# Two of the sixteen last stores of a fused attention and expert kernel begun from GpSimd's queue

## Chip, cores, metric

One core of a Trainium2 chip. The metric is the device time of one execution in microseconds (us). The profile's span (first to last recorded instruction) is about 1.8 us shorter than it (496.21 and 494.4 for the profiled run before), and all times in views are counted from the span's start.

## The reference, cut

```python
def _attn_ref(q, k, v):                     # q, k, v: (8, 8, 576, 64)
    q_p, k_p = phi(q), phi(k)               # phi(x) = elu(x) + 1
    kv = np.einsum('bhsd,bhse->bhde', k_p, v)
    num = np.einsum('bhsd,bhde->bhse', q_p, kv)
    den = np.einsum('bhsd,bhd->bhs', q_p, k_p.sum(2))[..., None] + 1e-06
    return num / den

def _moe_ref(x, domain_probs, w1, w2):      # x: (4608, 512), 4 experts of 512 -> 1024 -> 512
    p = domain_probs / (domain_probs.sum(-1, keepdims=True) + 1e-09)
    out = 0
    for e in range(4):
        out += p[:, e:e + 1] * (np.maximum(x @ w1[e], 0.0) @ w2[e])
    return out                              # (4608, 512) float32
```

## The kernel before, where the change touches it

Each batch has 576 tokens: four blocks of 128 and 64 left over. The left-over tokens of the eight batches form a ninth group of 512 tokens, the last "unit" with expert 3. Its second layer is seven products per half of the tokens (`p`, in the order 1, 2, 6, 5, 7, 3, 4; `i` is 0 or 1). Each product ends in one VectorE sum into `acc`. Products 2, 7, 3 and 4 complete a quadrant of the output: 128 tokens by 256 of the 512 columns. A quadrant holds rows of two batches, so it is stored by two DMAs of 64 partitions, one on SyncE's queue and one on ScalarE's: sixteen stores of 64 KB in all.

```python
    def store(j, ns, cols=slice(0, Dm)):
        acc = accs[j, ns][:, cols]
        if j < B:
            ...                              # whole blocks, on SyncE alone
        else:
            for u in range(2):
                (nc.scalar if u else nc.sync).dma_start(
                    out=out_b[2 * ns + u, SM:S, cols],
                    in_=acc[u * HP : (u + 1) * HP],      # HP = 64
                )

    def layer2_product(j, e, h, hss, p, i):
        ...                                  # 4 matmuls into PSUM
        add_acc(j, e, ns, ps, ds, first and e == 0)      # VectorE
        if (j, e) == (NTILES - 1, E - 1):
            if p in (2, 3, 4, 7):
                store(j, ns, ds)
```

## Time and profile before

| | before |
|---|---|
| median of the first 3 runs (all) | 495.89 us (495.54 to 497.17) |
| span of the profiled run, granted share of the full TensorE clock | 494.4 us, 1.0 |
| VectorE's last sum ends | 490.00 us |
| ScalarE's last store begins, lands | 491.32, 493.33 us |
| from VectorE's last end to the span's end ("the tail") | 4.4 us |

The lines that carry this stand in the prediction below. A line of the timeline such as `488.02 3.85 ACTq ... x6` merges six store issues of ScalarE's queue, from the first one's beginning at 488.02 over 3.85 us to the last one's end. Time in such a line is issue, not the transfer.

### The profile page before, as it was taken

To read this page: it belongs to the slowest core of one execution; us is meant where nothing else is said; L and a number is where in the kernel's file an instruction comes from. 1 tells how busy PE (TensorE), PEld (TensorE's weight loads), DVE (VectorE), ACT (ScalarE), POOL (GpSimd) and SP (SyncE) were. 2 spreads that over 40 slices of the span, in tenths; PEclk is the share of its full clock that TensorE was granted. 3 is DMA by queue.
4 is the path that set the end of the run, shared out by engine and by line. 5 is a ranking of instruction groups with operands and counts; after the bars stand their busy time and mean duration, and the time that the engine had idled before them with its cause. 6 is when DMAs were issued, how large, how long until landed. Compare 5 with 4: busy or idle time off the path is not lost.

```text
span 494.4 us, 11616 instructions
## 1 busy us (share of the span) xinstructions
PE 483.2 (98%) x4346; PEld 409.4 (83%) x4346; DVE 378.7 (77%) x802; ACT 336.2 (68%) x678; POOL 354.2 (72%) x339
## 2 busy tenths in 40 slices
PE   8999989999999999999999999999999999999995
PEld 3556656888898989898989898989898888888884
DVE  5757987798967987698859886888687756775686
ACT  5777969964978498848894789468954565446530
POOL 3735204778967797769776977698669877987774
PEclk9999999999999999999999999999999999999999
DMA  8999976542345235533464245523241020002003
GB/s 253 215 219 239 272 140 177 172 104 52 121 162 130 55 111 164 131 66 95 137 160 82 71 150 139 101 60 93 81 78 30 5 95 1 1 2 86 1 1 87
DMA packets 82201, 53.66 MB, mean 109 GB/s; under 512 B 46240, under 2 KB 75936, under 8 KB 82144
## 3 DMA queue, kind: packets, MB, share of 16 engines
q1 hardware_dynamic: 70592, 40.07, 30.7%
q0 software_dynamic: 9824, 11.27, 12.1%
q10 hardware_dynamic: 1728, 1.57, 1.2%
q8 instruction: 34, 0.56, 0.5%
q14 instruction: 23, 0.19, 0.1%
HBM read 45.16 MB, written 9.44 MB: 110 GB/s over the span
## 4 chain that ended last, share of the span: by engine, by line
PE 78%; DMA 12%; DVE 3%; ACT 3%; POOL 2%; issue 1%; SPq 0%; ACTq 0%; DVEq 0%; POOLq 0%
PE py L668 37%; PE pb L733 21%; PE pe L733 16%; DMA w<-in_moe_w_dram 7%; DMA rawu<-in_q_dram 2%; DVE acc L570 1%; PE psum_nd L465 1%; DMA rawb<-in_v_dram 1%; PE psum_kv L425 1%; PE py L579 1%; DMA out_dram<-acc 1%; DMA rawh<-in_q_dram 1%; POOL w L183 1%; PE pb L668 1%; DVE x_sb L448 1%
## 5 line engine op out<-in xcount | busy, mean ns | idle before, releaser
L570 DVE SCALAR_TENSOR_TENSOR acc<-py,p_sb,acc 128x256 f32<-128x256 f32 (+1 forms) x382 | 182.3, 488 | 49.4 <-PE py L668 40.1
L717 DVE CUSTOM_DVE_ANT_0 h<-pe,u 128x512 f16<-128x512 f32 x140 | 96.3, 688 | 42.0 <-PE pe L733 25.2
L733 PEld LDWEIGHTS <-w 128*128 128x128 f16 x1120 | 108.8, 98 | 17.0 <-issue 1.8
L635 POOL TENSOR_TENSOR hs<-h 128x512 f16<-128x512 f16 x64 | 73.9, 1155 | 55.2 <-DVE h L717 54.0
L668 PEld LDWEIGHTS <-h 128*128 128x128 f16 x1024 | 99.6, 98 | 12.3 <-issue 1.0
L668 PE MATMUL py<-w,h 128*128 128x256 f16 x744 | 106.4, 273 | 0.3 <-ACT acc L568 0.3
L744 ACT COPY u<-pb 128x512 f32<-128x512 f32 x140 | 82.7, 590 | 27.4 <-PE pb L733 25.8
L637 POOL TENSOR_TENSOR hs<-hs,h 128x512 f16<-128x512 f16 x64 | 74.6, 1166 | 27.2 <-PE py L668 24.6
L733 PEld LDWEIGHTS <-s 128*128 128x128 f16 x840 | 81.6, 98 | 11.4 <-DVE s L607 0.2
L733 PE MATMUL pb<-tt,w 128*128 128x256 f16 x560 | 84.0, 273 | 0.8 <-ACT u L744 0.7
L668 PEld LDWEIGHTS <-hs 128*128 128x128 f16 x768 | 74.4, 98 | 9.9 <-issue 1.3
L641 POOL TENSOR_TENSOR hs<-h,hs 128x512 f16<-128x512 f16 x64 | 74.4, 1162 | 3.5 <-PE py L668 2.9
L668 PE MATMUL py<-t,hs 128*128 128x256 f16 x496 | 74.4, 272 | 0.6 <-DVE acc L570 0.4
L639 POOL TENSOR_TENSOR h<-h 128x512 f16<-128x512 f16 x64 | 74.4, 1162 | 0.0
L759 ACT ACTIVATE h<-pe 128x512 f16<-128x512 f32 x70 | 41.9, 598 | 45.0 <-PE pe L733 44.5
L753 ACT COPY pe<-pb 128x512 f32<-128x512 f32 x70 | 40.2, 575 | 41.5 <-PE pb L733 14.9
L777 ACT ACTIVATE h<-pb 128x512 f16<-128x512 f32 x70 | 41.9, 599 | 10.0 <-PE pb L733 9.9
L733 PE MATMUL pb<-tt,s 128*128 128x256 f16 x280 | 42.0, 273 | 0.0
L733 PE MATMUL pe<-tt,s 128*128 128x256 f16 x280 | 42.0, 273 | 0.0
L733 PE MATMUL pb<-xT,w 128*128 128x256 f16 x248 | 37.2, 273 | 0.1
L733 PE MATMUL pe<-xT,w 128*128 128x256 f16 x248 | 37.2, 273 | 0.0
L733 PE MATMUL pe<-xT,s 128*128 128x256 f16 x248 | 37.2, 273 | 0.0
(120 smaller groups left out, 604.9 us busy)
## 6 DMA issues: line engine op xcount, KB each, us to landing
out_dram<-acc SPq DMA_DIRECT2D x32, 256.0 KB, 2.5
w<-in_moe_w_dram POOLq DMA_DIRECT2D x14, 512.0 KB, 13.0
rawb<-in_v_dram SPq DMA_DIRECT2D x26, 256.0 KB, 2.7
rawb<-in_q_dram SPq DMA_DIRECT2D x26, 256.0 KB, 2.7
rawb<-in_k_dram SPq DMA_DIRECT2D x26, 256.0 KB, 3.1
w<-in_moe_w_dram POOLq DMA_DIRECT2D x4, 256.0 KB, 5.8
rawb<-in_k_dram POOLq DMA_DIRECT2D x4, 256.0 KB, 11.1
rl<-in_q_dram SPq DMA_DIRECT2D x16, 64.0 KB, 2.5
```

The lines of the kernel that those rows point to most:

```text
L570: nc.vector.scalar_tensor_tensor(out=acc, in0=ps, scalar=pscal, in1=acc, op0=AO.mult, op1=AO.add)
L635: nc.gpsimd.tensor_tensor(out=hs[0], in0=a21, in1=a22, op=AO.add)
L637: nc.gpsimd.tensor_tensor(out=hs[1], in0=hs[0], in1=a11, op=AO.subtract)
L639: nc.gpsimd.tensor_tensor(out=a21, in0=a11, in1=a21, op=AO.subtract)
L641: nc.gpsimd.tensor_tensor(out=hs[3], in0=a12, in1=hs[1], op=AO.subtract)
L668: nc.tensor.matmul(out=ps, lhsT=lhsT(k), rhs=rhs[:, k], start=first and k == 0, stop=k == FH - 1, skip_group_check=True,)
L717: nc.vector._custom_dve(TENSOR_ADD_SAT, out=out, in0=ps, in1=u, s0=BIG, s1=0.0)
L733: nc.tensor.matmul(out=ps[:, kk], lhsT=lk(kc), rhs=rhs[:, kc], start=first and kk == 0 and kc == 0, stop=kc == 1, skip_group_check=True,)
L744: nc.scalar.copy(u, self.b)
L753: nc.scalar.copy(self.e5, self.b)
L759: nc.scalar.activation(self.h[:, :, 0, 0:NH], self.e5, AF.Relu)
L777: nc.scalar.activation(self.h[:, :, 1, 0:NH], self.b, AF.Relu)
```

## The change

Its intent: at the end the two hardware queues are behind VectorE, so one quadrant is taken off both and given to GpSimd, which is idle by then.

```diff
-    def store(j, ns, cols=slice(0, Dm)):
+    def store(j, ns, cols=slice(0, Dm), engs=(nc.sync, nc.scalar)):
@@
             for u in range(2):
-                (nc.scalar if u else nc.sync).dma_start(
+                engs[u].dma_start(
@@
             if p in (2, 3, 4, 7):
-                store(j, ns, ds)
+                store(j, ns, ds, *([(nc.gpsimd,) * 2] if (p, i) == (7, 1) else ()))
```

The built programs differ in nothing else: seven stores instead of eight on SyncE and on ScalarE, two new ones at the end of GpSimd's stream.

## The prediction

> **What bounds the kernel now.** I read the page's busy table first, then the timeline of the last ten microseconds, then the store issues one queue at a time, then the landings and SyncE's own waits.
>
> ```profile
> span 494.4 us, 11616 instructions
> PE 483.2 (98%) x4346; PEld 409.4 (83%) x4346; DVE 378.7 (77%) x802; ACT 336.2 (68%) x678; POOL 354.2 (72%) x339
> ```
>
> TensorE is busy in 98% of the span, so for some 489 us only TensorE's work counts. The change touches nothing there: the comparison of the two built programs finds TensorE's and VectorE's instruction streams identical. What can move is the tail after the last matmul. Its timeline, first VectorE's end, then the two store queues, each read again from a later moment so that the merged line splits:
>
> ```profile
> 489.08 0.92 DVE L570 SCALAR_TENSOR_TENSOR acc<-pb,p_sb,acc 128x256 f32<-128x256 f32 x2
> ...
> 485.22 6.29 SPq L557 DMA_DIRECT2D out_dram<-acc  x8
> 487.84 3.68 SPq L557 DMA_DIRECT2D out_dram<-acc  x6
> 490.97 0.55 SPq L557 DMA_DIRECT2D out_dram<-acc  x1
> ...
> 485.23 6.64 ACTq L557 DMA_DIRECT2D out_dram<-acc  x8
> 488.02 3.85 ACTq L557 DMA_DIRECT2D out_dram<-acc  x6
> 491.32 0.55 ACTq L557 DMA_DIRECT2D out_dram<-acc  x1
> ```
>
> The last sums are written at 490.00 (489.08 + 0.92). ScalarE's queue begins its last store only at 491.32, so it is 1.3 us behind the data. From the third store (488.02) to the eighth (491.32) are five steps: 3.30 / 5 = 0.66 us each; on SyncE 3.13 / 5 = 0.63. The issue itself takes 0.55 us, the rest is a wait instruction and gaps. VectorE delivers a quadrant every 0.44 us (two of 0.48, overlapping, in 0.92), so in this stretch the queues are the slower side. They hold the tail.
>
> ```profile
> L557 SPq DMA_DIRECT2D out_dram<-acc x4: 547/550/552, 489.0 to 491.0; - x4
> L557 ACTq DMA_DIRECT2D out_dram<-acc x4: 552/552/559, 489.4 to 491.3; - x4
> ...
> DMA to landing us min/median/max: 2.0/2.0/2.1
> ...
> SPq L1023 <- DMA out_dram<-acc: 1.5, 3, 0.6
> ```
>
> These are the last four stores of each queue: 2.0 us from issue to landing, with no growth from first to last, so the DMA engines are not backed up. The last lands at 491.32 + 2.01 = 493.33 (the trace's completion stamp), and SyncE's closing waits follow it (the last line). From there to the span's end it is 494.4 - 493.3 = 1.1 us of closing waits and barriers.
>
> The path of the end is therefore: VectorE's quadrants, ScalarE's queue at 0.66 us a store, 2.0 us of landing, 1.1 us of closing.
>
> **What the Trainium skill says.** "DMA: Bandwidth & Descriptors", section "Issuing engines are not separate DMA queues": all three issuers run on the same 16 DMA engines, and a second issuer saves only the time that a sequencer takes to initiate. That is just what is short here: 0.55 us of issue against 0.44 us of production. In "Latency and other measured facts" the same page gives a first byte after about 1 us for software descriptors and about 0.6 us for hardware ones. The trace agrees with the second: in steady state the first packet follows the end of a store's issue by 0.65 us. For GpSimd it is slower than stated: the first GpSimd load began at 10.43, took 0.91 us, and the software queue's first packet is at 12.78, 2.35 us after the start, though on DMA engines that other loads kept full. "Perfetto Trace Analysis", section "DMA Instruction — SWDGE (GPSIMD)": the recorded end of such an instruction is the end of descriptor writing, not of the data. I count it so.
>
> **The change, part by part.** The fourth of the eight quadrants in store order (the second token block of product 7) moves. Its two halves of 64 partitions x 256 columns (64 KB each) leave SyncE and ScalarE, which keep seven stores each, and go one after the other to GpSimd, whose last compute ends at 487.13 (485.97 + 1.16) and which is then free.
>
> - Removed: one store from each hardware queue. ScalarE's third store stays at 488.02 to 488.63. The next is now the first quadrant of product 3, whose data are complete at 488.69 (the end of the fourth record before the end; 490.00 less three steps of 0.44), so it begins at about 488.71: queue and data meet. Four stores remain, three steps of 0.65 after it: 488.71 + 1.95 = 490.66 for the last, against 491.32. That is 0.66 us gained; its landing goes from 493.33 to about 492.67. SyncE's last comes to 490.64, so both queues end together.
> - Added: two issues on GpSimd. Their data are complete at 488.25. GpSimd's load issues of 64 KB (the leftover rows) took 0.63 to 0.65 us, the first issue of the run 0.91. From 488.30 I take 0.91 and 0.65: ends at 489.2 and 489.85. First packets 1.44 us later (12.78 - 11.34, from the one case above): 490.65 and 491.3. From first packet to landing a steady store takes 0.8 us (492.53 to 493.33): landings at 491.45 and 492.1. This is an estimate, and about 0.6 us of slack to 492.67.
> - Moved: completion counters. The hardware stores use eight counters in turn; with 14 stores instead of 16 the last ones fall on counters that SyncE checks earlier in its closing series. Each check takes 0.06 us, and about two more now stand after the last landing: +0.12 us.
> - Contention: in the steady part the DMA engines are 0.90 busy at 204 GB/s (490.0 to 491.9), and two stores are to be fitted into a tail that is shorter by 0.66 us. Early in the run they moved 340 GB/s, so busy is not full, but I allow 0.1 us.
>
> Sum: -0.66 + 0.12 + 0.1 = -0.44 us, so a span of 494.0 and, taken from the median, 495.89 - 0.44 = 495.45 us. That is 0.1% of the time.
>
> **Rivals.**
>
> - GpSimd's stores become the last to land. Each queue's first two stores after a rest landed 3.1 to 3.6 us after issue, against 2.0 later, and ScalarE's second issue lasted 2.09 us. A rested software queue may pay the same: 1.4 us more puts its landings at 492.85 and 493.5, past the hardware's 492.67 and even past the old 493.33. The end would then be the same or up to 0.4 us later: 495.9 to 496.3. GpSimd idles from 487.13 and has issued no DMA since about 52 us, which speaks for this; that the 2.35 us already came from a first use on full engines speaks against. I give it 35%.
> - The issue is not the limit, the DMA engines are (0.90 busy). Then fewer stores per queue bring no earlier end, since the bytes are the same: 495.9. Against it speaks the constant 2.0 us to landing; a backed-up engine would make it grow. 10%.
> - Everything meets: no contention, no extra closing checks, the full 0.66 us: 495.2. 15%.
>
> What is left, 40%, is the main line. All of these lie within 0.15% of each other's neighbour; the spread of the three runs before (495.54 to 497.17) is larger than any of them.
>
> **Range and chances.** The cases run from 495.2 to 496.3; with the runs' scatter, 494.7 to 496.7. Two per cent would be 9.9 us. The whole tail after the last matmul is about 5 us, so faster by 2% is excluded, and slower by 2% would need something outside the tail or the slow luck of one chip. Faster 0.005, same 0.985, slower 0.01.
>
> **What would show it.** In the changed profile: seven stores a queue, ScalarE's last beginning near 490.66 with a landing of 2.0; two GpSimd issues from about 488.3, of 0.6 to 0.9 us; a software-queue row with 128 KB in the tail, first packet near 490.6; the last TensorE and VectorE records where they were. Wrong would be: a landing of the GpSimd stores after 492.7; landings of the hardware stores growing beyond 2.1 us (contention); a closing of clearly more than 1.2 us (GpSimd's own drain or counters); a third hardware store later than 488.1, which would mean that the slow second issue on ScalarE changed too.

## The result, and the profile after

| | before | after |
|---|---|---|
| median of 6 runs each (all) | 496.06 us (495.54 to 497.17) | 496.14 us (495.65 to 496.37) |
| five rounds: median | 496.17 us of 9 | 495.87 us of 5 |
| tail, profile of the first job / second profile | 4.44 / 4.42 us | 4.09 / 4.13 us |

The ratio of after to before is 0.9998 (95% interval 0.9985 to 1.0011) in the first job and 0.9989 (0.9976 to 1.0003) in the five rounds. A ratio is the mean time of one kernel's fast runs over that of the other's of the same rounds, so it is not quite the ratio of the medians quoted. Kernels are compared only within the same rounds.

The page of the changed kernel, first lines; TensorE is as busy as before:

```profile
span 494.2 us, 11615 instructions
...
PE 483.7 (98%) x4346; PEld 409.7 (83%) x4346; DVE 378.4 (77%) x802; ACT 336.6 (68%) x678; POOL 355.8 (72%) x341
```

The timeline of its last microseconds, with the two hardware queues each read from more than one moment (start, length, engine, what, how many):

```profile
489.21 0.92 DVE L570 SCALAR_TENSOR_TENSOR acc<-pb,p_sb,acc 128x256 f32<-128x256 f32 x2
488.68 1.13 POOL L557 DMA_DIRECT2D out_dram<-acc  x2 [1.41 <-DVE acc L570]
487.98 3.27 SPq L557 DMA_DIRECT2D out_dram<-acc  x5
490.69 0.56 SPq L557 DMA_DIRECT2D out_dram<-acc  x1
487.98 3.58 ACTq L557 DMA_DIRECT2D out_dram<-acc  x5
488.85 0.52 ACTq L557 DMA_DIRECT2D out_dram<-acc  x1
489.47 0.77 ACTq L557 DMA_DIRECT2D out_dram<-acc  x1
491.00 0.56 ACTq L557 DMA_DIRECT2D out_dram<-acc  x1
```

VectorE ends at 490.13 (489.21 + 0.92), 0.13 us later than in the profile before, so I count from there. ScalarE's last store begins at 491.00, 0.87 us after VectorE's end; before it was 1.32. Two things in these lines were not forecast. GpSimd begins its first store at 488.68, though its data were complete at 488.38 (the end of a VectorE sum). And one of ScalarE's issues, at 489.47, takes 0.77 us where 0.55 is usual.

The landings of the stores still at issue after 489.6, from the view of the output tensor (us from issue to landing):

```profile
DMA to landing us min/median/max: 2.0/2.3/2.5
```

In the kernel before the last eight stores landed 2.0 to 2.1 us after issue; here they take 2.0 to 2.5. The last hardware store is again a 2.02 (to 493.02); the longer ones come before it. GpSimd's two landed 1.95 and 2.40 us after issue, at 490.63 and 491.64. Their rows went out in 32 packets of 4096 bytes in all, where one store of a hardware queue took 64 of 1024 bytes. The Trainium skill, "DMA: Bandwidth & Descriptors", section "Anatomy of one DMA — SWDGE (gpsimd) path", gives about 2.0 us of fixed cost for a software DMA; these landings agree.

From the trace's completion stamps, the tail is this sum, in us after VectorE's last end:

```
                  last store begins   lands    closing until the span's end   tail
before                 1.32           3.33              1.11                  4.44
after                  0.87           2.89              1.20                  4.09
```

So the tail is 0.35 us shorter in the first pair of profiles, and 0.29 in the second pair (4.42 and 4.13).

### The profile page after: what moved, and what is told of

Its sections match the earlier page's. It is cut to its first block, busy times and chain, and to the rows that moved or that the text cites. A ratio compares the mean times of both kernels' runs of the same rounds, so it can differ in the third digit from the quotient of the medians.

```text
span 494.2 us, 11615 instructions
## 1 busy us (share of the span) xinstructions
PE 483.7 (98%) x4346; PEld 409.7 (83%) x4346; DVE 378.4 (77%) x802; ACT 336.6 (68%) x678; POOL 355.8 (72%) x341
## 3 DMA queue, kind: packets, MB, share of 16 engines
q10 hardware_dynamic: 1648, 1.51, 1.1%
## 4 chain that ended last, share of the span: by engine, by line
PE 81%; DMA 10%; DVE 3%; ACT 3%; POOL 1%; issue 1%; DVEq 0%; POOLq 0%; ACTq 0%
PE py L668 38%; PE pb L733 22%; PE pe L733 16%; DMA w<-in_moe_w_dram 7%; DMA rawu<-in_q_dram 2%; PE warm_ps L860 1%; PE psum_nd L465 1%; DMA rawb<-in_v_dram 1%; PE psum_kv L425 1%; DVE acc L570 1%; DVE x_sb L448 1%; PE pb L668 1%; PE py L579 0%; ACT u L744 0%; ACT psum_ee L315 0%
## 5 line engine op out<-in xcount | busy, mean ns | idle before, releaser
L668 PE MATMUL py<-w,hs 128*128 128x256 f16 x248 | 37.2, 273 | 0.0
```

The lines of the kernel that those rows point to most:

```text
L668: nc.tensor.matmul(out=ps, lhsT=lhsT(k), rhs=rhs[:, k], start=first and k == 0, stop=k == FH - 1, skip_group_check=True,)
```

## Experiments

My theory A, after the result: the tail is a chain of issues on the hardware queues, 2.0 us of landing and a closing series (SyncE's checks of the completion counters, then barriers of all engines); the change shortens the chain, by less than forecast; and 0.3 us is too small to be seen in whole runs. The rivals: the shorter tail is luck; the DMA engines and not the issues are the limit; GpSimd's stores slow the hardware queues.

Times below are in us after VectorE's last end in the same trace unless a clock time is meant. A queue's "step" is the time from the beginning of one issue to the beginning of the next.

**before_again**: no edit.

> The kernel before, unchanged, for a second profile: how far the tail (from VectorE's last end to the span's end, 4.4 us in the first profile) repeats on its own, and where the scatter of whole runs (495.5 to 497.2) lies. Theory A (the tail is a fixed chain of issues; the scatter is earlier, in the loads of the first microseconds): tail 4.3 to 4.5 us, the last store's issue 1.3 us after VectorE's end. Rival (the tail itself scatters by as much as the change moved it, so the 0.35 us seen are luck): a tail below 4.2 us.

```profile
488.53 0.92 DVE L570 SCALAR_TENSOR_TENSOR acc<-pb,p_sb,acc 128x256 f32<-128x256 f32 x2
490.76 0.55 ACTq L557 DMA_DIRECT2D out_dram<-acc  x1
```

In its timeline VectorE ends at 489.45 and ScalarE's last store begins at 490.76, 1.31 later; the tail is 4.42 (4.44 in the first profile). The tail repeats to 0.02 us. The spans differ by 0.5 us (494.4 and 493.9), all of it before the tail. Counting VectorE's records in both traces, the difference is 0.55 us at the 250th (156 us) and 0.55 us at the last; before that it changes its sign, from 0.57 us later to 0.55 us earlier than the first trace. In all fourteen traces each one's offset from the first at the 250th record is its offset at the last within 0.02 us. Over these traces VectorE's last end lies between 489.37 and 490.72: that is the scatter in which 0.3 us disappears.

**after_again**: no edit, five rounds.

> The changed kernel, unchanged. Theory A: tail 4.0 to 4.2 us (4.1 in the first profile), GpSimd's stores land about 2.0 and 2.4 us after issue and well before the hardware queues' last; whole time 0.3 us below the kernel before, which five rounds may not separate from zero. Rival (luck): tail anywhere in 4.0 to 4.5.

```profile
488.98 0.92 DVE L570 SCALAR_TENSOR_TENSOR acc<-pb,p_sb,acc 128x256 f32<-128x256 f32 x2
487.75 3.56 ACTq L557 DMA_DIRECT2D out_dram<-acc  x5
489.24 0.76 ACTq L557 DMA_DIRECT2D out_dram<-acc  x1
490.76 0.55 ACTq L557 DMA_DIRECT2D out_dram<-acc  x1
```

The tail is 4.13, with the same slow issue (0.76) and the last store at 490.76 - 489.90 = 0.86. Luck as the source of the shorter tail is unlikely: 4.09 and 4.13 here, 4.44 and 4.42 in the two traces of the kernel before. The whole time is 0.9989 of before, interval 0.9976 to 1.0003: as expected, not separable from 1.

**half_bytes** (wrong result):

```diff
-                    out=out_b[2 * ns + u, SM:S, cols],
-                    in_=acc[u * HP : (u + 1) * HP],
+                    out=out_b[2 * ns + u, SM:S, cols][:, 0 : DH // 2],
+                    in_=acc[u * HP : (u + 1) * HP, 0 : DH // 2],
```

> Wrong result on purpose: the kernel before with each of the last unit's stores cut to half its columns (64 rows of 512 bytes instead of 1024), as many issues. Theory A (issue on the two queues is the limit): issue step stays 0.63 to 0.66 us, the last store begins 1.3 us after VectorE's last end, the tail shortens by 0.2 us at most, from the shorter transfer itself: 4.2 to 4.4 us. Rival (the DMA engines are the limit, as their 0.90 busy share suggests): the step falls to VectorE's 0.44 us, the last store begins right after the last sum, tail about 3.3 us.

```profile
488.96 0.92 DVE L570 SCALAR_TENSOR_TENSOR acc<-pb,p_sb,acc 128x256 f32<-128x256 f32 x2
489.87 1.85 ACTq L557 DMA_DIRECT2D out_dram<-acc  x3
491.17 0.55 ACTq L557 DMA_DIRECT2D out_dram<-acc  x1
```

Half the bytes, and ScalarE's last three issues are still 0.65 apart ((491.17 - 489.87) / 2), the last one 1.29 after VectorE's end, as before. The landing shrinks from 2.01 to 1.86 and the tail from 4.43 to 4.26. Bytes are not what limits the kernel before. The packets were as many as before, only smaller; that the DMA engines are not the limit either is shown by one_queue below.

**drop_quad** (wrong result): the moved quadrant is not stored at all.

```diff
-            if p in (2, 3, 4, 7):
+            if p in (2, 3, 4, 7) and (p, i) != (7, 1):
```

> Wrong result on purpose: the kernel before with the fourth quadrant (product 7, second token block) not stored at all, so seven stores a hardware queue and none on GpSimd. It is the ceiling of the change. Theory A: ScalarE's last store begins 0.66 us after VectorE's last end (the sum of the prediction) and lands at 2.67; tail 3.8 to 3.9 us (before 4.43, changed kernel 4.09 to 4.13); all steps 0.64 to 0.66 and all landings 2.0 to 2.1. The 0.2 us between this and the changed kernel's 0.86 is then GpSimd's stores in the way of the hardware queues. Rival (seven stores a queue take 0.2 us more for a reason of their own, such as the third store or the counters): last store at 0.85, landing at 2.9, tail 4.1 as in the changed kernel.

```profile
488.45 0.92 DVE L570 SCALAR_TENSOR_TENSOR acc<-pb,p_sb,acc 128x256 f32<-128x256 f32 x2
488.09 0.52 ACTq L557 DMA_DIRECT2D out_dram<-acc  x1
488.71 0.76 ACTq L557 DMA_DIRECT2D out_dram<-acc  x1
490.24 0.55 ACTq L557 DMA_DIRECT2D out_dram<-acc  x1
```

Here theory A failed on a number and the rival was right. Without any GpSimd store the same issue takes 0.76 us, the last store begins at 490.24 - 489.37 = 0.87, lands at 2.91, and the tail is 4.13: that of the changed kernel. So GpSimd's two stores cost nothing at the end, and the slow issue is not their doing. What both kernels share is that the two hardware queues, both empty, begin a store within 0.01 us of each other (1.28 before VectorE's end, the first quadrant of product 3), and ScalarE's next store begins 0.06 after SyncE's next. In the kernel before ScalarE runs about 0.33 us behind SyncE through this stretch; it had slipped to that offset over its third and fourth stores (issues of 0.61 us).

The slip is no peculiarity of these two kernels. In ten of the fourteen traces (all but pool_two, one_dma, one_queue and half_rows) the last stores of the two queues begin 0.29 to 0.35 us apart, which is half of the 0.64 us step. The offset arises in one issue of 0.76 to 0.88 us, or in two or three of 0.59 to 0.70, after the queues have begun a store within 0.2 us of each other; in pool_early it is SyncE that falls behind.

**act_half**: only ScalarE's half of the quadrant moves.

```diff
-                store(j, ns, ds, *([(nc.gpsimd,) * 2] if (p, i) == (7, 1) else ()))
+                store(j, ns, ds, *([(nc.sync, nc.gpsimd)] if (p, i) == (7, 1) else ()))
```

> Only one half of the moved quadrant goes to GpSimd, in place of ScalarE; SyncE keeps its eight stores, ScalarE has seven. Theory A (each queue by itself is held by its own issues): ScalarE's last begins near 0.7 us after VectorE's last end, SyncE's stays at 0.9 to 1.0 as before, landing 2.0 later, so the last landing comes at about 3.0 us (before 3.33, changed kernel 2.89), tail 4.1 to 4.2. It also tests whether ScalarE's slow issue in the changed kernel (0.77 us where 0.55 is usual, at the time of GpSimd's second issue) comes with two GpSimd issues: with one I expect no such issue. Rival (the two queues share one issue resource, so that moving one half frees both): SyncE's last begins 0.3 us earlier too.

```profile
486.37 2.11 SPq L557 DMA_DIRECT2D out_dram<-acc  x1
488.57 3.76 SPq L557 DMA_DIRECT2D out_dram<-acc  x6
```

ScalarE's last store begins at 0.96. SyncE's begins at 1.28 and lands at 3.28, and the tail is 4.49: no gain at all, where 4.1 to 4.2 was expected. SyncE's last does not begin earlier than before (0.97), so the rival, that moving one half frees both queues, is not seen. The number failed since in this run SyncE's second store, at 4.13 before the end, took 2.11 us (0.55 and 1.70 in the two traces of the kernel before) and made its third late by 0.22 (1.93 before the end in place of 2.16). From there SyncE keeps its steps of 0.64. There is a slow ScalarE issue (0.88) here too, with one GpSimd store, where none was expected. What it is worth to relieve one queue alone stays open: had SyncE's last begun at 0.97 as before, the tail would have been about 4.2 (an estimate: 0.97, 2.02 of landing and this run's closing of 1.21). The run was not repeated.

**pool_early**: the second quadrant moves instead of the fourth.

```diff
-                store(j, ns, ds, *([(nc.gpsimd,) * 2] if (p, i) == (7, 1) else ()))
+                store(j, ns, ds, *([(nc.gpsimd,) * 2] if (p, i) == (2, 1) else ()))
```

> The quadrant given to GpSimd is the second (product 2, second token block), which the hardware queues store while they have time to spare, in place of the fourth. Theory A (only a store that stands in the queue after 487.8 is worth anything): last store 1.3 us after VectorE's end, tail 4.3 to 4.5 us as before, in spite of the seven stores a queue. GpSimd's stores begin when its last sum ends, near 2.8 us before VectorE's end, and its drain ends 1.5 us after the landing of its last store, that is near 1.5 to 2 us, hidden. Rival (what counts is the number of stores on a queue): tail 4.1 us. Rival on the drain (it ends a fixed time after the closing begins, whatever its stores do): drain at 3.0 us again.

```profile
488.86 0.76 SPq L557 DMA_DIRECT2D out_dram<-acc  x1
```

SyncE's last store begins at 1.34 and the tail is 4.53. Here SyncE has the slow issue and ends behind ScalarE (1.05). Seven stores a queue are worth nothing if the one taken away had time to spare. GpSimd's drain ended at 1.22, not at 3.0, and 1.6 after its last landing at -0.39, which speaks for a drain that follows the landing.

**pool_last**: the eighth quadrant moves.

```diff
-                store(j, ns, ds, *([(nc.gpsimd,) * 2] if (p, i) == (7, 1) else ()))
+                store(j, ns, ds, *([(nc.gpsimd,) * 2] if (p, i) == (4, 1) else ()))
```

> The quadrant given to GpSimd is the very last one (product 4, second token block) instead of the fourth. If a GpSimd store is as quick from data to landing as the changed kernel's trace shows (0.3 us late to start, 0.57 us an issue, 2.0 and 2.4 us to landing), the second lands 3.3 us after VectorE's last end, where the kernel before has 3.33: tail 4.3 to 4.5 us, and GpSimd's landing ends the chain while ScalarE's last lands near 2.7. The rival that a rested software queue is slow (first landing 3.5 us or more after issue, as the first stores of the hardware queues) would make it 5.3 us or more.

**pool_two**: the fourth and the sixth quadrant move, five rounds.

```diff
-                store(j, ns, ds, *([(nc.gpsimd,) * 2] if (p, i) == (7, 1) else ()))
+                store(j, ns, ds, *([(nc.gpsimd,) * 2] if (p, i) in ((7, 1), (3, 1)) else ()))
```

> Two quadrants go to GpSimd: product 7 and product 3, each second token block, four issues in all; six stores are left on each hardware queue. Theory A: the last hardware stores begin 0.2 to 0.4 us after VectorE's last end (the data of product 4 hold them, at 0.44 us a quadrant, then one step of 0.65), landing at 2.2 to 2.4; GpSimd's fourth issue begins near 0.3 us after VectorE's end and lands 2.4 later, at 2.7: tail 3.8 to 3.9 us, whole time 0.5 us below before. Rival (GpSimd's issues slow the hardware queues, as the 0.77 us suggests): the hardware steps grow to 0.75 or more and the tail stays at 4.1.

Both were misses, for one reason. GpSimd's timeline of pool_last, then of pool_two:

```profile
488.68 0.92 DVE L570 SCALAR_TENSOR_TENSOR acc<-pb,p_sb,acc 128x256 f32<-128x256 f32 x2
489.89 1.13 POOL L557 DMA_DIRECT2D out_dram<-acc  x2 [3.16 <-DVE acc L570]
```

```profile
488.91 0.92 DVE L570 SCALAR_TENSOR_TENSOR acc<-pb,p_sb,acc 128x256 f32<-128x256 f32 x2
488.38 2.16 POOL L557 DMA_DIRECT2D out_dram<-acc  x4 [1.41 <-DVE acc L570]
490.02 0.78 ACTq L557 DMA_DIRECT2D out_dram<-acc  x1
```

In pool_last GpSimd begins at 0.30 and its second store lands at 3.26, as expected. ScalarE's last lands at 3.45 and not near 2.7: it took 2.72 from issue, with GpSimd's transfers beside it. Neither explains the tail of 5.56, where 4.3 to 4.5 was expected. In pool_two the last hardware store begins at 0.20, as expected, lands at 3.28 (3.08 after its issue, instead of 2.0 to 2.1, with GpSimd's transfers beside it) and the tail is 5.25. Whole time 1.0014 of before (1.0001 to 1.0028). What ends both is GpSimd's own closing drain. Its records, from the traces (an ordinary listing, us after VectorE's last end):

```
             GpSimd's last landing   its drain ends   difference   tail
pool_early          -0.39                1.22            1.61       4.53
act_half             0.82                2.31            1.48       4.49
after                1.51                3.03            1.52       4.09
after_again          1.56                3.08            1.52       4.13
pool_two             2.86                4.46            1.60       5.25
pool_last            3.26                4.78            1.52       5.56
```

Without GpSimd stores this drain ends with VectorE's last sum (at 490.00 in the kernel before). With them it ends 1.5 to 1.6 us after the landing of its last store, and 0.8 us of barriers follow it (5.25 - 4.46 and 5.56 - 4.78). In the changed kernel SyncE's side of the closing is done at 3.34, so the drain at 3.03 is hidden by 0.3 us. The chosen quadrant is thus near the latest that can be given to GpSimd; the next one, 0.44 us later, was not tried.

**one_dma**: no GpSimd, both halves of a quadrant in one store, on alternating queues, five rounds.

```diff
-            for u in range(2):
-                (nc.scalar if u else nc.sync).dma_start(
-                    out=out_b[2 * ns + u, SM:S, cols],
-                    in_=acc[u * HP : (u + 1) * HP],
-                )
+            eng = (nc.sync, nc.scalar)[turn_st[0] % 2]
+            turn_st[0] += 1
+            eng.dma_start(out=out_b[2 * ns : 2 * ns + 2, SM:S, cols], in_=acc)
```

> No GpSimd: the two halves of each quadrant in one store of 128 KB (three-dimensional destination), alternating between SyncE and ScalarE, so eight issues in all instead of sixteen and the same bytes. Theory A: each queue now issues every 0.87 us of data and keeps up; the last store begins within 0.1 us of VectorE's last end and lands 2.0 to 2.4 us after: tail 3.2 to 3.6 us, whole time 0.9 us below before (0.2%). Rival (issue time grows with the rows of the store, 1.1 us for 128): no gain, tail 4.2 to 4.5 us. Rival (DMA engines): tail 4.4.

Time 512.49 us, 1.0337 of before (1.0323 to 1.0351), with a tail of 20.88, for a reason that none of the three expectations had. The DMA view of 490 to 510 us:

```profile
DMA  1111111111111111111111111111111111111110
DMA packets 935, 0.94 MB, mean 47 GB/s; under 512 B 16, under 2 KB 935, under 8 KB 935
```

The DMA engines are 0.1 busy on average, at 47 GB/s. The packets under 512 B are the counter writes of the completions: 16 here for the eight stores, two for each, where the kernel before has 256 for its sixteen, sixteen for each. So two of the sixteen DMA engines carried each store. The Trainium skill says why, in "DMA: Bandwidth & Descriptors", section "Why a DMA increments its semaphore by 16 and not by 1": the number of engines is the largest one up to 16 that divides the slowest dimension of both sides, and the destination here has a slowest dimension of 2 (two batches). The trace agrees.

**full_rows**: no GpSimd, fewer and larger late stores, five rounds.

```diff
-            if p in (2, 3, 4, 7):
-                store(j, ns, ds)
+            if p in (2, 3, 4):
+                store(j, ns, *(() if p == 4 else (ds,)))
```

> No GpSimd: product 7's quadrants are not stored by themselves; the last product's store takes the whole row of 512 columns of its token block (64 rows of 2048 bytes) instead. Six stores a queue, the same bytes, a correct result. Theory A (the number of late issues is what counts): the first of the last four begins when product 3's data are complete, 1.3 us before VectorE's last end, the last 0.66 us after it; its larger landing takes 2.1 to 2.4 us, so 2.8 to 3.1: tail 3.9 to 4.2 us, as good as the changed kernel without GpSimd. Whole time 0.2 to 0.5 us below before, not separable from zero. Rival (the DMA engines bound the end once half of the bytes come last): last landing at 3.3 or later, tail 4.4 or more.

ScalarE's last store begins at 0.86, but with 2048-byte rows it lands 2.50 after issue, at 3.36, and the closing takes 1.35: tail 4.71. Time 1.0015 of before (1.0001 to 1.0029). The rival's numbers held; its cause, the DMA engines, is not shown by that. The closing is the longer since the last store of twelve falls on a counter that SyncE checks almost first: seven checks of 0.06 us follow it, five in the changed kernel, and three in the kernel before.

**one_queue**: all sixteen on SyncE.

```diff
-                (nc.scalar if u else nc.sync).dma_start(
+                nc.sync.dma_start(
```

> The kernel before with all sixteen last stores on SyncE's queue and none on ScalarE's. It measures what an issue costs with no other queue at work. Theory B (the two queues get in each other's way: 0.47 us alone, 0.55 in turn, 0.76 and more where both begin together): issues of 0.47 to 0.52 us throughout, a step near 0.56 us, and no issue over 0.6 but that of the instruction fetch near 4 us before VectorE's end. With twelve stores from 2.16 us before VectorE's last end the last begins near 4.0 us after it. Rival (an issue costs 0.55 us of its own, 0.76 has another cause): step 0.63 to 0.65 as before, the last store near 4.9 us. Third case (a shared resource that serves one issue per 0.32 us whichever queue asks): step near 0.32 to 0.4, last store at 1.4 to 2.2.

```profile
487.29 8.85 SPq L557 DMA_DIRECT2D out_dram<-acc  x14
```

Issues of 0.55 and 0.59 us in turn, a step of 0.64 (8.26 us from the first beginning to the last, over 13 steps), the last store at 6.06. (The expectation counted twelve stores from there instead of fourteen.) The tail is 9.14 and the whole time 500.49 us in this one look. Theory B's 0.47 us for an issue alone falls, the rival's step stands: 0.64 us is the queue's own and not the price of a second queue. The DMA engines are 0.45 busy from 490 to 495 us, against 0.82 from 488.4 to 491.5 in the kernel before, and the step is the same, so they are not its limit. There is no issue above 0.6 us after the second store, which leaves open that the slow issues come from two queues that begin together.

**half_rows** (wrong result): drop_quad with 32 of 64 rows in each store.

```diff
-                    out=out_b[2 * ns + u, SM:S, cols],
-                    in_=acc[u * HP : (u + 1) * HP],
+                    out=out_b[2 * ns + u, SM : SM + HP // 2, cols],
+                    in_=acc[u * HP : u * HP + HP // 2],
```

> Wrong result on purpose: the kernel without the fourth quadrant's stores, each other store of the last unit cut to 32 of its 64 rows (half the packets, each of the same 1024 bytes). It asks what makes ScalarE slip to 0.86 us in one step when both queues start together, 1.28 us before VectorE's last end. Theory C (the two queues share a stage that takes about 0.32 us for a store of 64 rows, in proportion to rows): no slip, every ScalarE issue at 0.5 to 0.6 us, last ScalarE store at 0.66 us after VectorE's end or earlier. Rival (the slip has nothing to do with rows: a fixed price of issuing at the same moment): again one ScalarE issue of 0.75 us or more, last store near 0.87. The issue's own step: 0.64 us again if its cost is fixed, 0.4 to 0.5 if it goes with rows.

```profile
489.80 0.92 DVE L570 SCALAR_TENSOR_TENSOR acc<-pb,p_sb,acc 128x256 f32<-128x256 f32 x2
489.44 1.79 ACTq L557 DMA_DIRECT2D out_dram<-acc  x4
490.86 0.38 ACTq L557 DMA_DIRECT2D out_dram<-acc  x1
```

With 32 rows an issue takes 0.32 to 0.38 us and a step 0.47 ((490.86 - 489.44) / 3), close to VectorE's 0.44. No ScalarE issue is slow, the last begins at 0.14, the tail is 3.01. This fits theory C, but does not prove it: SyncE now waits for the data (it begins 0.03 to 0.05 us after each sum) and ScalarE falls behind by about 0.03 us a store only, so the test of two queues that both run late is gone.

## Why the prediction was right, step by step

- **What bounds, and that the result is "same": right.** The time stays inside the range, the change is in the tail alone, and half_bytes and one_queue confirm the reading that the issue step of 0.64 us is the queue's own and that it, not bytes, holds the end. The range of 2 us is far wider than the 0.44 us forecast, so the whole time tests little of the mechanism; the tail does.
- **ScalarE's last store, forecast 0.66 us after VectorE's end: 0.87.** The step that failed is "three steps of 0.65 after it": measured 0.61, 0.86 and 0.67. The term was taken from a stretch in which the queues were already offset by 0.33 us; with the quadrant gone they restart together and ScalarE slips to that offset again, 0.2 us late. drop_quad shows that this comes from the shortened hardware queues alone. A likely reason is in the Trainium skill, "Perfetto Trace Analysis", section "DMA Instruction — HWDGE (DVE, Sync)": the descriptor generator is one block that a sequencer locks for its own use, and the recorded issue includes the wait for the lock. The traces fit it in so far as the queues settle 0.29 to 0.35 us apart, half a step, and one queue alone has no such slip. No run isolates the lock, so this cause stays argued.
- **GpSimd's stores, forecast to land at 1.45 and 2.1 after VectorE's end: 0.50 and 1.51, so hidden, as said.** The terms were wrong one by one: it began 0.30 us after its data instead of 0.05, needed 0.57 for each issue instead of 0.91 and 0.65, and its first packet followed the issue's end by 0.57 (489.82 after 489.25) instead of 1.44. The 1.44 had been measured on DMA engines that were full. From the start of the issue the first packet came after 1.14 us, close to the 1 us of the Trainium skill's page that the prediction cites. The prediction compared GpSimd's packet from the start of its issue with a hardware queue's from the end; counted alike, from the start, a hardware store's first packet comes after 1.2 us in the kernel before, so GpSimd is not the slower. That the stores were hidden was luck in part: with a landing at the forecast 2.1 and a drain 1.52 us behind it, GpSimd would have been done at 3.62, after SyncE's 3.34, and the tail would have been about 4.4 as before (an estimate, with the 0.78 from the drain to the span's end in pool_two and pool_last).
- **Counters, forecast +0.12: +0.10** (closing 1.20 against 1.11 before; 1.22 and 1.11 in the second profiles).
- **Contention, forecast +0.1: none at the end.** Landings of 2.2 to 2.5 in the middle, but the last at 2.02, and drop_quad without GpSimd ends no earlier. Where GpSimd's transfers run beside the last hardware store it is real: 2.72 for that landing in pool_last and 3.08 in pool_two.
- **Sum, forecast -0.44: -0.35 and -0.29 in the two pairs of tails.** The whole-run medians show +0.08 in one job and -0.30 in the other; the scatter covers it, as the prediction expected, and the traces place that scatter in the first 160 us.
- **Rivals.** A rested software queue as the last to land: no, its landings took 1.95 and 2.40 us. Its drain, which the prediction named only as a sign of error, is the real limit, 0.3 us away. The DMA engines as the limit: no (half_bytes, one_queue). The full 0.66: no.

What stays open: the cause of the slip, why GpSimd begins 0.3 us after its data, what relieving one queue alone is worth, and whether the changed kernel is faster in whole runs. The best estimate is the tail's 0.3 us of 496, 0.06%. No other version with a correct result beats it: pool_two and full_rows are 0.14 to 0.15% slower than before.

## What to carry to other kernels

When a kernel's end is held by a queue of small stores, count issues and steps, not bytes, and ask which store stands in the queue at the end: only taking away one of those was worth anything here. Two queues that issue at the same time ended half a step apart, so allow for that. A store on GpSimd was about as quick as a hardware one (1.95 to 2.45 us from issue to landing in the changed kernel), but it must land about 1.5 us before the rest of the closing, because GpSimd's final drain waits that long after it. For a gain of a fraction of a microsecond read the tail in a profile; whole runs will not show it.

## What the Trainium skill lacked or had wrong

- No page has the closing drain of GpSimd: it ended 1.48 to 1.61 us after the landing of GpSimd's last store in six traces, and held the end in two of them (tails 5.25 and 5.56 us in place of 4.4).
- "DMA: Bandwidth & Descriptors", section "Issuing engines are not separate DMA queues", calls the time to initiate a DMA usually small relative to the DMA. Here it sets the tail: 0.55 us of issue, 0.64 us a step, for stores that land in 2.0 us.
- No page gives the issue time of a hardware queue by shape for this chip. Stores of 32 rows took 0.32 to 0.38 us to issue, those of 64 rows 0.47 to 0.52 after a wait for data and 0.55 in a row, and this kernel's stores of 128 rows of 2048 bytes on SyncE a median of 0.36: not monotone in the rows.
- No page has this: the second store of one or both hardware queues took 1.5 to 2.1 us to issue in ten of the fourteen traces, when a 16 KB instruction-fetch packet was under way, and its issue ended about 0.4 us after that packet (487.98 after 487.58 in the kernel before). This was seen, not tested.
- No page has the offset of two hardware queues that issue back to back: their last stores of 64 rows began 0.29 to 0.35 us apart in ten traces, at a step of 0.64.
